# The 1e-9 of two softmaxes as a summed place, and pooled keys and values written once instead of twice

## The chip, the cores and the metric

The kernel runs on one core of a Trainium2 chip. The metric is the device time of one execution in microseconds (us); shorter is better. Five engines work side by side, each through its own queue of instructions in order: TensorE (PE in the profile, its weight loads PEld), VectorE (DVE), ScalarE (ACT), GpSimd (POOL) and SyncE (SP), which here issues the DMAs. They meet at semaphores.

## What is computed

Attention over pooled keys and values, then a soft mixture of experts, then an MLP with a squared ReLU. The change touches the first part and the first normalisation of the second:

```python
k_p = k.reshape(B, H, Sp, 8, D).mean(axis=3)          # B=8, H=8, S=576, Sp=72, D=64
v_p = v.reshape(B, H, Sp, 8, D).mean(axis=3)
scores = (1 / sqrt(D)) * q @ k_p^T                    # 72 scores for each query and head
attn = exp(scores - scores.max(-1))
attn = attn / (attn.sum(-1) + 1e-9)
x = attn @ v_p                                        # 4608 tokens x 512
...
logits = x @ phi                                      # 4608 x 32 slots
d = exp(logits - logits.max(0)); d /= d.sum(0) + 1e-9 # over all tokens
slot_input = d.T @ x                                  # 32 slots, into 8 experts w1, w2
...
x = softmax(logits, over slots) @ slot_out
out = (s * relu(x @ w_in)**2 + b) @ w_out             # 4608 x 512
```

## The kernel before

**Stages.** The program has three parts in time. The attention part, to about 217 us, works on tiles of 128 query rows: four pairs of batch entries (`pr` 0 to 3), nine tiles (`u` 0 to 8) in each, 36 in all. The expert part, to about 265 us, streams `w1` and `w2` through the 32 slot rows. The MLP part runs to the end; it is nearly all matmuls of line 1073. Nothing of the change lies behind the first line of the expert part.

**One tile of attention** goes through stages that the loop calls by letters. `st_A` transposes the queries (L353, ACT copy L355). `st_B` makes the scores (L383 into PSUM tile `sc`), DVE takes the row maximum (L390) and subtracts it into `S` (L393). `st_C` lets ACT take the exponential in place (L397); DVE sums each of the 8 rows of 72 (L401 into `sm`), adds 1e-9 (L402), takes the reciprocal (L404); POOL multiplies `S` by it into the probabilities `P` (L421). `st_D` transposes `P` on PE (L434, L435), `st_E` makes the logits (L457, L464), `st_F` brings them into `L_t` (L480, L482).

**Order.** The order is written by hand: for each step `t` a string of letters in `LOOP` or `FIRST` says in which order the stages of different tiles are put down, and each engine runs its own instructions in that order. A tile's B comes two steps behind its A, C one behind that, D two further on, E and F behind that. `r` advances a `dispatch` generator (the sums over tokens of one batch entry, L538 to L623), `p` a `prep` generator.

**Pooling the keys and values** (`pool_chunk`) is what `prep` runs for the next pair while a pair is worked on, by the table `PLAN1` or `PLAN2`: each pair has three chunks of k and three of v, each handed to DVE or POOL. A chunk is three adds of halves: 512 places to 256 (L246), 256 to 128 (L250), 128 to 64 (L251). The last writes each sum twice, side by side, `[128, 3, 2, 64]`, through a repeated read. `kv_transpose` then transposes 128 columns at a time (L264), so that the same 64 rows stand in the upper and in the lower half of a PSUM bank, and ACT copies the upper half into rows 0 to 63 of `kb_t` (L273) or `vt` (L285) and the lower half into rows 64 to 127. The end of a chunk's third add frees the buffer of the load, and SP can issue the next load into it. In all there are 24 chunks: 11 on DVE, 13 on POOL.

**The tail** of attention (`TAIL`) brings the last two batch entries' sums together: `merge_3` multiplies the three partial sums `z_3` by their weights (L521), adds them (L523), adds 1e-9 (L524), takes the reciprocal (L525) and scales (L526). The last `dispatch` needs that for L607, its matmuls L611 and the slot inputs `siz` (L623), with which the expert part starts at L939. At the end of the tail a buffer named `brief` becomes free for one more load of expert weights.

`S` is a tile of a pool with two buffers, allocated anew for each tile; a subtraction into it waits until POOL has read the tile before last.

Of the kernel before, what the change touches and what calls it, by code (L numbers as in the profile page):

```python
# [10 lines left out]
F32 = mybir.dt.float32  # L11
# [3 lines left out]
ALU = mybir.AluOpType  # L15
# [41 lines left out]
def kernel(  # L57
# [37 lines left out]
    m_all = cpool.tile([128, B, 32], F32, name="m_all")  # L95
    z_all = cpool.tile([128, B, 32], F32, name="z_all")
    si_sum = cpool.tile([128, 4, 32], F32, name="si_sum")
# [134 lines left out]
    for i in range(NPR):  # L232
        nc.gpsimd.memset(L_t[i], -3.0e38)

    pump()
    nc.scalar.activation(out=selrep[:, 0, 0:1], in_=ident[:, 0:1], func=ACTF.Exp)
# [6 lines left out]
    def pool_chunk(nm, pr, c, eng):  # L243

        x = where[nm, pr, c][2]
        eng.tensor_tensor(out=x[:, :, 0:256], in0=x[:, :, 0:256], in1=x[:, :, 256:512], op=ALU.add)  # L246
        yield
        if (nm, pr) not in kvp:
            kvp[nm, pr] = pp1.tile([128, 9, 2, D], F32, tag=f"{nm}p", name=f"{nm}p", bufs=1)
        eng.tensor_tensor(out=x[:, :, 0:128], in0=x[:, :, 0:128], in1=x[:, :, 128:256], op=ALU.add)  # L250
        eng.tensor_tensor(  # L251
            out=kvp[nm, pr][:, 3 * c:3 * c + 3],
            in0=x[:, :, 0:64].unsqueeze(2).to_broadcast([128, 3, 2, D]),
            in1=x[:, :, 64:128].unsqueeze(2).to_broadcast([128, 3, 2, D]),
            op=ALU.add,
        )
        done((nm, pr, c))

    def kv_transpose(nm, pr, c):
# [3 lines left out]
        for i in range(3):  # L263
            nc.tensor.transpose(  # L264
                out=ps[:, 128 * i:128 * i + 128],
                in_=src[:, 3 * c + i].rearrange("p t d -> p (t d)"),
                identity=ident,
            )
        if nm == "k":
            for h2 in range(2):  # L270
# [3 lines left out]
                    out=o.rearrange("p n (g u) -> p g n u", g=3),  # L274
                    in_=ps[r, 0:384].rearrange("p (g n u) -> p g n u", g=3, u=8),
                    func=ACTF.Copy, scale=1.0 / 64,
# [4 lines left out]
        for h2 in range(2):  # L281
            r = slice(64 * h2, 64 * h2 + 64)
            o = vt_t[pr][r].rearrange("p b c x -> p (b c) x")[:, :, 24 * c:24 * c + 24]
            i_ = ps[r, 0:384].rearrange("p (g n t u) -> p g n t u", g=3, n=8, t=2)[:, :, :, h2, :]
            nc.scalar.activation(out=o.rearrange("p n (g u) -> p g n u", g=3), in_=i_, func=ACTF.Copy, scale=1.0 / 8)  # L285
# [79 lines left out]
    def st_B(t):  # L365
# [24 lines left out]
        nc.vector.tensor_reduce(out=mx, in_=scv, axis=AX.X, op=ALU.max)  # L390
        S = sc2.tile([128, 2, 4, KP], F32, tag="S", name="S", bufs=2)
        S_t[t] = S
        nc.vector.tensor_tensor(out=S, in0=scv, in1=mx.unsqueeze(3).to_broadcast([128, 2, 4, KP]), op=ALU.subtract)  # L393

    def st_C(t):
        S = S_t[t]
        nc.scalar.activation(out=S, in_=S, func=ACTF.Exp)  # L397
        pr, u = divmod(t, 9)
        S = S_t.pop(t).rearrange("p x i k -> p (x i) k")
        sm = ap2.tile([128, 8], F32, tag="sm", name="sm")  # L400
        nc.vector.tensor_reduce(out=sm, in_=S, axis=AX.X, op=ALU.add)  # L401
        nc.vector.tensor_scalar(out=sm, in0=sm, scalar1=1e-9, scalar2=None, op0=ALU.add)  # L402
        rs = ap2.tile([128, 8], F32, tag="rs", name="rs")
# [115 lines left out]
    def merge_3():  # L519

        nc.vector.tensor_tensor(out=z_3, in0=z_3, in1=m_3, op=ALU.mult)  # L521
        zt = ap2.tile([128, 32], F32, tag="zd", name="zt")
        nc.vector.tensor_reduce(out=zt, in_=z_3.rearrange("p b s -> p s b"), axis=AX.X, op=ALU.add)  # L523
        nc.vector.tensor_scalar(out=zt, in0=zt, scalar1=1e-9, scalar2=None, op0=ALU.add)  # L524
        nc.vector.reciprocal(out=zt, in_=zt)  # L525
# [672 lines left out]
```

## Time and profile before

| | |
|---|---|
| time before, median of 3 runs | 719.14 us (719.0 to 721.34) |
| the profiled execution | 724.16 us; its span 722.0 us, 2.16 us lie around it |
| PE busy, of the span | 665.4 us (92%) |
| DVE busy | 499.0 us (69%) |
| ACT busy | 411.4 us (57%) |
| POOL busy | 297.3 us (41%) |
| mean granted clock of TensorE | 0.956 of full speed |

The span is the time from the first to the last instruction. The shares of busy time are means over parts with different limits: DVE is busy for 69% of the whole and for 70% to 86% of the attention part. A row of the time line gives start, length, engine, line, operation and tile, and in square brackets how long the engine sat idle before it and what ended that. A row of the chain of waits gives start, length and the instruction to which the end of the program can be followed back. The clock column gives 1.00 for 2.4 GHz and 0.50 for 1.2 GHz.

### The profile page before, as it was taken

How to read it: one execution, taken by the hardware profiler on the slowest of the kernel's cores; microseconds unless marked ns; L12 is line 12 of the kernel's file. 1: busy time of each engine (PE TensorE's matmuls, PEld its weight loads, DVE VectorE, ACT ScalarE, POOL GpSimd, SP SyncE). 2: the span in 40 equal slices, each digit the busy share in tenths (PEclk: the TensorE clock that was granted, in tenths of full speed). 3: DMA queues.
4: the chain of work that ended last, by engine and by line, in shares of the span. 5: the costliest groups of instructions: out<-in, count | busy, mean ns of one | idle time of the engine just before them, and what ended most of it. 6: DMA issues, size and time to landing. Idle time of an engine off the chain costs nothing.

```text
span 722.0 us, 11198 instructions
## 1 busy us (share of the span) xinstructions
PE 665.4 (92%) x4294; PEld 522.2 (72%) x4294; DVE 499.0 (69%) x805; ACT 411.4 (57%) x714; POOL 297.3 (41%) x221
## 2 busy tenths in 40 slices
PE   4677889899899978999999999999999999999997
PEld 3566767677763337778888888878788888888885
DVE  6768788667766297788776797888665765456443
ACT  3454666566433345877566666666665666555552
POOL 3646656532210054356132543345331433899100
PEclk9786999899878997999999999999999999999999
DMA  8997446545296980111011110121100000122322
GB/s 302 376 327 223 177 155 198 196 155 203 94 381 241 391 293 33 59 32 58 28 59 59 59 58 1 53 66 59 59 1 0 1 1 1 63 98 90 99 89 88
DMA packets 41317, 88.87 MB, mean 123 GB/s; under 512 B 6960, under 2 KB 15152, under 8 KB 41264
## 3 DMA queue, kind: packets, MB, share of 16 engines
q1 hardware_dynamic: 41264, 88.16, 35.3%
q8 instruction: 34, 0.56, 0.3%
q14 instruction: 19, 0.16, 0.1%
HBM read 78.71 MB, written 9.44 MB: 122 GB/s over the span
## 4 chain that ended last, share of the span: by engine, by line
PE 73%; DVE 16%; ACT 4%; DMA 2%; POOL 2%; issue 2%; SPq 1%; DVEq 0%; POOLq 0%; ACTq 0%
PE o L1073 52%; PE h L1016 4%; PE sc L383 3%; DVE S L393 2%; DVE mx L390 2%; DVE sm L401 2%; PE l L939 2%; DMA ring<-in_v_dram 1%; PE w L434 1%; ACT S L397 1%; PE w L601 1%; PE so_ps L947 1%; DMA brief<-in_moe_w_dram 1%; PE w L578 1%; PE ct L898 1%
## 5 line engine op out<-in xcount | busy, mean ns | idle before, releaser
L1073 PE MATMUL o<-whi,gh 128*128 128x512 f32 x576 | 229.4, 399 | 2.5 <-DVE gh L1043 2.5
L1073 PE MATMUL o<-whi,gl 128*128 128x512 f32 x576 | 225.5, 392 | 0.8 <-DVE gl L1044 0.7
L1073 PE MATMUL o<-wlo,gh 128*128 128x512 f32 x576 | 225.6, 392 | 0.0
L1025 ACT ACTIVATE r<-h 128x768 f32<-128x768 f32 x95 | 77.2, 813 | 152.7 <-PE h L1016 149.0
L1044 DVE TENSOR_TENSOR gl<-r,gh 128x768 fp32r<-128x768 f32 (+1 forms) x97 | 114.5, 1181 | 63.2 <-ACT gh L1033 62.8
L1086 DVE SCALAR_TENSOR_TENSOR part<-o,sb_t,part 128x512 f32<-128x512 f32 x144 | 99.6, 743 | 50.4 <-PE o L1073 47.8
L1073 PEld LDWEIGHTS o<-whi,gh 128*128 128x128 f32 x576 | 108.8, 189 | 24.1 <-issue 5.8
L1073 PEld LDWEIGHTS o<-wlo,gh 128*128 128x128 f32 x576 | 108.7, 189 | 24.1
L1073 PEld LDWEIGHTS o<-whi,gl 128*128 128x128 f32 x576 | 108.8, 189 | 21.6 <-DVE gl L1044 2.8
L831 POOL TENSOR_TENSOR fr<-fr,xp 128x512 f32<-128x512 f32 x28 | 41.1, 1467 | 183.3 <-ACT fr L830 161.2
L1026 ACT ACTIVATE r<-r 128x768 f32<-128x768 f32 x95 | 80.5, 847 | 3.0
L1033 ACT CAST gh<-r 128x768 fp32r<-128x768 f32 x95 | 79.5, 836 | 2.4
L421 POOL TENSOR_TENSOR P<-S,rs 128x576 f32<-128x576 f32 x32 | 37.3, 1166 | 82.9 <-DVE rs L404 42.0
L1167 POOL TENSOR_TENSOR part<-part,wsum 128x512 f32<-128x512 f32 x36 | 53.3, 1521 | 10.5 <-ACT wsum L1161 10.5
L1016 PE MATMUL h<-cT,S 128*128 128x384 f32 x192 | 49.7, 342 | 0.5 <-DVE S L859 0.5
L383 PE MATMUL sc<-kb,qT 128*128 128x144 f32 x256 | 44.3, 325 | 0.0
L832 POOL TENSOR_TENSOR th<-th,fr 128x512 f32<-128x512 f32 x28 | 43.0, 1537 | 2.2
L1016 PEld LDWEIGHTS h<-cT,S 128*128 128x128 f32 x192 | 36.7, 192 | 8.2 <-DVE S L859 0.7
L390 DVE TENSOR_REDUCE mx<-sc 128x8 f32<-128x576 f32 x36 | 26.4, 734 | 20.6 <-PE sc L383 17.3
L383 PEld LDWEIGHTS sc<-kb,qT 128*128 128x128 f32 x256 | 40.0, 223 | 0.4 <-ACT qT L355 0.2
L401 DVE TENSOR_REDUCE sm<-S 128x8 f32<-128x576 f32 x36 | 27.0, 750 | 18.3 <-ACT S L397 18.2
L397 ACT ACTIVATE S<-S 128x576 f32<-128x576 f32 x36 | 24.5, 682 | 25.2 <-DVE S L393 25.2
(211 smaller groups left out, 910.2 us busy)
## 6 DMA issues: line engine op xcount, KB each, us to landing
ring<-in_moe_w_dram SPq DMA_DIRECT2D x14, 1024.0 KB, 7.6
x<-in_moe_w_dram SPq DMA_DIRECT2D x13, 1024.0 KB, 9.8
raw<-in_moe_w_in_dram SPq DMA_DIRECT2D x8, 1024.0 KB, 5.6
raw<-in_moe_w_out_dram SPq DMA_DIRECT2D x8, 1024.0 KB, 4.9
out_dram<-part SPq DMA_DIRECT2D x32, 256.0 KB, 2.5
ring<-in_q_dram SPq DMA_DIRECT2D x7, 1024.0 KB, 9.6
ring<-in_v_dram SPq DMA_DIRECT2D x9, 768.0 KB, 9.8
ring<-in_k_dram SPq DMA_DIRECT2D x7, 768.0 KB, 7.0
```

Of the source, the lines that this page charges most:

```text
L383: nc.tensor.matmul(out=sc[:, i // 2, 2 * KP * (i % 2):2 * KP * (i % 2) + 2 * KP], lhsT=qT[:, i, :], rhs=kb[:, H * bb + 4 * (j % 2) + i, :] ...
L401: nc.vector.tensor_reduce(out=sm, in_=S, axis=AX.X, op=ALU.add)
L831: nc.gpsimd.tensor_tensor(out=fr, in0=fr, in1=xp, op=ALU.mult)
L832: nc.gpsimd.tensor_tensor(out=th if dst is None else dst, in0=th, in1=fr, op=ALU.add)
L1016: nc.tensor.matmul(out=h[x][:, 0:384] if i == 0 else h[:, x, 0:384], lhsT=Sw_t[f], rhs=cT(c, 384), start=True, stop=True)
L1025: nc.scalar.activation(out=r, in_=h[:, :, 0:384], func=ACTF.Relu)
L1026: nc.scalar.activation(out=r, in_=r, func=ACTF.Square)
L1033: nc.scalar.copy(out=gh_t[i], in_=r)
L1044: nc.vector.tensor_tensor(out=gl[:, x], in0=r[:, x], in1=gh[:, x].bitcast(F32), op=ALU.subtract)
L1073: nc.tensor.matmul(out=o_t[tt], lhsT=l[:, x, 128 * c:128 * c + 128], rhs=r, start=(fi == 0 and n == 0), stop=(fi == GROUPS[g] - 1 and n == 2),
L1086: nc.vector.scalar_tensor_tensor(out=p, in0=o_t[tt], scalar=sb_t[:, 0:1], in1=p, op0=ALU.mult, op1=ALU.add)
L1167: nc.gpsimd.tensor_tensor(out=p, in0=p, in1=wsum, op=ALU.add)
```

## The change

There are two parts. In the first, each row of `S` gets a 73rd place that holds 1e-9. Two fixed buffers of 8 rows of 73 are allocated once and taken in turn; a memset writes the 73rd places at the start, and the subtraction, the exponential and the product touch the first 72 only. The sum takes all 73, so the add of 1e-9 (L402) is gone. In the same way the token sums `z_all` get one more entry that holds 1e-9, `merge_3` adds four entries instead of three, and L524 is gone. In the second, the third add of a chunk writes each sum once, `[128, 3, 64]`; the transposes take 64 columns and fill rows 0 to 63 of the bank, and ACT copies these rows twice: to rows 0 to 63 and to rows 64 to 127. The numbers of copies, transposes and adds stay.

```diff
-    z_all = cpool.tile([128, B, 32], F32, name="z_all")
+    z_all = cpool.tile([128, B + 1, 32], F32, name="z_all")
...
+    S_buf = [sc2.tile([128, 2, 4, KP + 1], F32, name=f"S{i}", bufs=1) for i in range(2)]
+    for S in S_buf:
+        nc.vector.memset(S[:, :, :, KP:KP + 1], 1e-9)
+    nc.vector.memset(z_all[:, B], 1e-9)
...
-            kvp[nm, pr] = pp1.tile([128, 9, 2, D], F32, tag=f"{nm}p", name=f"{nm}p", bufs=1)
+            kvp[nm, pr] = pp1.tile([128, 9, D], F32, tag=f"{nm}p", name=f"{nm}p", bufs=1)
...
         eng.tensor_tensor(
-            out=kvp[nm, pr][:, 3 * c:3 * c + 3],
-            in0=x[:, :, 0:64].unsqueeze(2).to_broadcast([128, 3, 2, D]),
-            in1=x[:, :, 64:128].unsqueeze(2).to_broadcast([128, 3, 2, D]),
-            op=ALU.add,
+            out=kvp[nm, pr][:, 3 * c:3 * c + 3], in0=x[:, :, 0:64], in1=x[:, :, 64:128], op=ALU.add,
         )
...
             nc.tensor.transpose(
-                out=ps[:, 128 * i:128 * i + 128],
-                in_=src[:, 3 * c + i].rearrange("p t d -> p (t d)"),
-                identity=ident,
+                out=ps[0:64, 128 * i:128 * i + 128], in_=src[:, 3 * c + i], identity=ident,
             )
...
-                    in_=ps[r, 0:384].rearrange("p (g n u) -> p g n u", g=3, u=8),
+                    in_=ps[0:64, 0:384].rearrange("p (g n u) -> p g n u", g=3, u=8),
...
-            i_ = ps[r, 0:384].rearrange("p (g n t u) -> p g n t u", g=3, n=8, t=2)[:, :, :, h2, :]
+            i_ = ps[0:64, 0:384].rearrange("p (g n t u) -> p g n t u", g=3, n=8, t=2)[:, :, :, h2, :]
...
-        S = sc2.tile([128, 2, 4, KP], F32, tag="S", name="S", bufs=2)
-        S_t[t] = S
-        nc.vector.tensor_tensor(out=S, in0=scv, in1=mx.unsqueeze(3).to_broadcast([128, 2, 4, KP]), op=ALU.subtract)
+        S_t[t] = S = S_buf[t % 2]
+        nc.vector.tensor_tensor(out=S[:, :, :, 0:KP], in0=scv, in1=mx.unsqueeze(3).to_broadcast([128, 2, 4, KP]), op=ALU.subtract)
...
+        Sk = S[:, :, 0:KP]
+        nc.scalar.activation(out=Sk, in_=Sk, func=ACTF.Exp)
         nc.vector.tensor_reduce(out=sm, in_=S, axis=AX.X, op=ALU.add)
-        nc.vector.tensor_scalar(out=sm, in0=sm, scalar1=1e-9, scalar2=None, op0=ALU.add)
+        S = Sk
...
-        nc.vector.tensor_reduce(out=zt, in_=z_3.rearrange("p b s -> p s b"), axis=AX.X, op=ALU.add)
-        nc.vector.tensor_scalar(out=zt, in0=zt, scalar1=1e-9, scalar2=None, op0=ALU.add)
+        nc.vector.tensor_reduce(out=zt, in_=z_all[:, B - 3:].rearrange("p b s -> p s b"), axis=AX.X, op=ALU.add)
```

DVE's queue in the first pair, around the softmax whose sum runs at 65.8 us (`ring_80` is the load of a v chunk of the next pair, `vp` the pooled v, `sc` the scores in PSUM, `w` a PSUM bank); before, and then now:

```order
L251 TENSOR_TENSOR vp<-ring_80 128x384
L482 TENSOR_REDUCE L_72<-w 128x64
L401 TENSOR_REDUCE sm<-S 128x8
L402 TENSOR_SCALAR sm<-sm 128x8
L404 RECIPROCAL rs<-sm 128x8
L390 TENSOR_REDUCE mx<-sc 128x8
L393 TENSOR_TENSOR S<-sc,mx 128x576
```

```order
L256 TENSOR_TENSOR vp<-ring_80 128x192
L482 TENSOR_REDUCE L_72<-w 128x64
L401 TENSOR_REDUCE sm<-S_131 128x8
L404 RECIPROCAL rs<-sm 128x8
L390 TENSOR_REDUCE mx<-sc 128x8
L392 TENSOR_TENSOR S_132<-sc,mx 128x8x72
```

The add of 1e-9 between sum and reciprocal is gone, the third add of the chunk has half the places, and the rest stands in the same order; `S` has become two named buffers.

DVE's queue at the end of the tail, from the copy of the last token sum on; before, and then now:

```order
L566 COPY z_all<-w 128x32
L521 TENSOR_TENSOR z_all<-z_all,m_all 128x96
L523 TENSOR_REDUCE zt<-z_all 128x32
L524 TENSOR_SCALAR zt<-zt 128x32
L525 RECIPROCAL zt<-zt 128x32
L526 TENSOR_TENSOR m_all<-m_all,zt 128x96
L621 COPY si_all<-w 64x128 x2
L607 TENSOR_TENSOR a<-w,m_all 72x256
```

```order
L565 COPY z_all<-w 128x32
L521 TENSOR_TENSOR z_all<-z_all,m_all 128x96
L523 TENSOR_REDUCE zt<-z_all 128x32
L524 RECIPROCAL zt<-zt 128x32
L525 TENSOR_TENSOR m_all<-m_all,zt 128x96
L620 COPY si_all<-w 64x128 x2
L606 TENSOR_TENSOR a<-w,m_all 72x256
```

One instruction of eight is gone; nothing else moved.

PE's queue in the first pair, around the transposes of a k chunk of the second pair that start at 54.2 us (`P_1` and `P_2` are probabilities, `LT` the logits before their transpose); before, and then now:

```order
L383 MATMUL sc<-kb_123,qT 128x144 x4
L434 MATMUL w<-ident,P_1_103 128x128 x4
L435 MATMUL w<-ident,P_1_103 64x128
L264 MATMUL w<-ident,kp 128x128 x3
L353 MATMUL w<-ident,qm 128x128 x4
```

```order
L383 MATMUL sc<-kb_123,qT 128x144 x4
L434 MATMUL w<-ident,P_1_103 128x128 x4
L435 MATMUL w<-ident,P_1_103 64x128
L266 MATMUL w<-ident,kp 64x128 x3
L353 MATMUL w<-ident,qm 128x128 x4
```

The three transposes give 64 rows instead of 128; their place is the same.

## Rows read from the trace of the kernel before

**Rows 1.** Busy time by stretch: PE, PEld, DVE, ACT, POOL, clock, DMA share, GB/s.

```profile
30.00:60.00 30.00, 24.04 (x213) 19.69 (x212) 20.49 (x38) 16.15 (x38) 13.96 (x12) 0.73 0.88 292
90.00:120.00 30.00, 25.18 (x311) 20.50 (x309) 25.89 (x50) 18.75 (x46) 16.81 (x14) 1.00 0.46 141
150.00:180.00 30.00, 28.66 (x395) 23.42 (x393) 21.62 (x49) 18.48 (x49) 8.05 (x7) 1.00 0.46 170
224.00:250.00 26.00, 26.00 (x202) 8.30 (x194) 8.31 (x27) 10.20 (x38) 0.13 (x1) 1.00 0.94 341
```

**Rows 2.** The chain of waits at the adds of 1e-9: start, length, instruction.

```profile
44.99 0.18 DVE sm L402
...
45.20 0.20 DVE rs L404
...
189.15 0.18 DVE sm L402
```

**Rows 3.** Time line of DVE: a chunk's adds while POOL is idle or past its reads.

```profile
32.88 0.95 DVE L246 TENSOR_TENSOR raw<-raw 128x768 f32<-128x768 f32 x1
34.46 0.56 DVE L251 TENSOR_TENSOR kp<-raw 128x384 f32<-128x384 f32 x1
```

**Rows 4.** Time line of POOL: the first and third add of a chunk.

```profile
47.73 1.00 POOL L251 TENSOR_TENSOR kp<-raw 128x384 f32<-128x384 f32 x1
...
78.70 1.80 POOL L246 TENSOR_TENSOR ring<-ring 128x768 f32<-128x768 f32 x1
```

**Rows 5.** Time lines of DVE and then POOL, both adding a chunk.

```profile
63.05 1.24 DVE L250 TENSOR_TENSOR ring<-ring 128x384 f32<-128x384 f32 x1
64.32 1.23 DVE L251 TENSOR_TENSOR vp<-ring 128x384 f32<-128x384 f32 x1
...
62.23 1.64 POOL L250 TENSOR_TENSOR ring<-ring 128x384 f32<-128x384 f32 x1
63.95 1.19 POOL L251 TENSOR_TENSOR vp<-ring 128x384 f32<-128x384 f32 x1
```

**Rows 6.** The chain of waits at the third adds.

```profile
21.16 1.19 POOL vp L251
...
117.79 1.24 DVE kp L251
...
148.29 1.14 POOL vp L251
```

**Rows 7.** Time line of PE: its waits for DVE and POOL, in brackets.

```profile
27.73 1.12 PE L434 MATMUL w<-ident,Pm 128*128 128x128 f32 x4 [4.30 <-POOL Pm L421]
...
54.21 0.87 PE L264 MATMUL w<-ident,kp 128*128 128x128 f32 x3 [3.12 <-DVE kp L251]
68.87 0.39 PE L545 MATMUL w<-ident,md 128*32 128x128 f32 x1 [4.57 <-DVE md L538]
82.17 0.52 PE L264 MATMUL w<-ident,kp 128*128 128x128 f32 x3 [1.94 <-ACT LT L469]
...
149.47 0.55 PE L264 MATMUL w<-ident,vp 128*128 128x128 f32 x3 [1.27 <-POOL vp L251]
```

**Rows 8.** Groups by line and form, weight loads: count, busy us, mean ns.

```profile
L434 PEld LDWEIGHTS w<-ident,P 128*128 128x128 f32 x128 | 16.7, 158 | 3.8 <-POOL P L421 2.5 <-ACT vps L297 0.4 <-issue 0.3
L435 PEld LDWEIGHTS w<-ident,P 128*64 128x64 f32 x32 | 4.0, 125 | 0.3 <-ACT qT L355 0.3
```

**Rows 9.** Groups by line and form: copies of ACT, and a strided sum of DVE.

```profile
L273 ACT ACTIVATE kb<-w 64x384 f32<-64x384 f32 x24 | 11.7, 488 | 11.7 <-PE w L264 11.5
L587 ACT COPY at<-w 128x288 f32<-128x288 f32 x16 | 6.3, 400 | 2.9 <-PE w L583 2.4
L538 DVE TENSOR_REDUCE md<-L 128x32 f32<-128x160 f32 x8 | 3.2, 406 | 0.1
```

**Rows 10.** The chain of waits at the end of attention.

```profile
212.83 0.19 DVE zt L524
...
216.74 6.72 DMA brief<-in_moe_w_dram
```

More of the change, by code (lines that the diff above doesn't have):

```diff
@@ L390, in st_B @@
         nc.vector.tensor_reduce(out=mx, in_=scv, axis=AX.X, op=ALU.max)
-        S = sc2.tile([128, 2, 4, KP], F32, tag="S", name="S", bufs=2)
-        S_t[t] = S
-        nc.vector.tensor_tensor(out=S, in0=scv, in1=mx.unsqueeze(3).to_broadcast([128, 2, 4, KP]), op=ALU.subtract)
+        S_t[t] = S = S_buf[t % 2]
+        nc.vector.tensor_tensor(out=S[:, :, :, 0:KP], in0=scv, in1=mx.unsqueeze(3).to_broadcast([128, 2, 4, KP]), op=ALU.subtract)
     def st_C(t):
-        S = S_t[t]
-        nc.scalar.activation(out=S, in_=S, func=ACTF.Exp)
+        S = S_t.pop(t).rearrange("p x i k -> p (x i) k")
         pr, u = divmod(t, 9)
-        S = S_t.pop(t).rearrange("p x i k -> p (x i) k")
         sm = ap2.tile([128, 8], F32, tag="sm", name="sm")
+        Sk = S[:, :, 0:KP]
+        nc.scalar.activation(out=Sk, in_=Sk, func=ACTF.Exp)
         nc.vector.tensor_reduce(out=sm, in_=S, axis=AX.X, op=ALU.add)
-        nc.vector.tensor_scalar(out=sm, in0=sm, scalar1=1e-9, scalar2=None, op0=ALU.add)
+        S = Sk
         rs = ap2.tile([128, 8], F32, tag="rs", name="rs")
```

## The prediction

> **What bounds the kernel now.** I read the busy times by stretch first. Between 90 and 120 us PE is busy for 25.2 of 30 us and DVE for 25.9; between 150 and 180 us PE stands at 28.7 and DVE at 21.6 [rows 1]. So no one engine sets the pace of the attention part: PE and DVE hand it to each other, and from about 150 us on PE holds it almost alone. From 224 to 250 us PE is busy without a gap [rows 1], and everything there starts from the slot inputs at the end of attention; the change leaves that part alone, so a gain or a loss in attention moves it as a block. The question is therefore how much earlier attention ends. For that I followed the chain of waits through its 217 us. It passes 17 of the 36 adds of 1e-9 (the first and the last in [rows 2]), nine of the 24 third adds (six on DVE, three on POOL, [rows 3, 5, 6]) and the add of the tail [rows 10]. Then I looked at PE's own waits [rows 7], since what DVE or POOL finish sooner is worth something only where PE would otherwise stand idle.
>
> **The change part by part.**
>
> *The 36 adds of 1e-9.* From the start of such an add to the start of the reciprocal behind it pass 45.20 - 44.99 = 0.21 us [rows 2]. All 36 are 7.6 us of DVE time; the 17 on the chain are 17 x 0.21 = 3.6 us. The sum takes 8 places more: a place costs (0.95 - 0.56) / (768 - 384) = 1.0 ns on DVE [rows 3], so 0.008 us, and 17 of them 0.14 us. The waits of the subtraction stay what they were, since two buffers taken in turn are what the pool gave, and the three memsets at the start stand in DVE's queue ahead of an instruction that waits for POOL anyway, while the first load is still on its way. I cost them at nothing; if that cover were gone they would be three tiny instructions once, under 0.21 us each by [rows 2].
>
> *The third adds.* On DVE 384 places take 0.56 us alone [rows 3], so 192 take 0.56 - 192 x 1.0 ns = 0.36, a gain of 0.20. On POOL a place costs (1.80 - 1.00) / 384 = 2.1 ns [rows 4], a gain of 0.40. When both add a chunk, both stretch: POOL's second add takes 1.64 instead of 1.00, DVE's second and third 1.24 and 1.23 instead of 0.56 [rows 3 to 5]. The ends tell why: DVE's second add ends 64.29, POOL's 63.87; DVE's third ends 65.55, POOL's 65.14. Both times DVE is 0.41 to 0.42 us behind the other's end: it waits for POOL's instruction and then does its own. With both third adds halved, such a pair gains on both sides, 0.40 + 0.20 = 0.6 us. Of the six DVE adds on the chain four are of that kind (1.23 to 1.25; [rows 5] and the 117.79 of [rows 6]) and two free: 4 x 0.6 + 2 x 0.2 = 2.8 us. The lower bound, if only DVE's own places counted, is 6 x 0.2 = 1.2. The three POOL adds on the chain (1.19 the first, 1.14 the last, [rows 6]) give 3 x 0.4 = 1.2.
>
> *Transposes and copies.* A weight load of 64 columns takes 125 ns, one of 128 columns 158 [rows 8]: 72 x 33 ns = 2.4 us of PEld, which runs beside the matmuls, and the moving side keeps its 128 columns. I take zero; the most it can give is the first load behind a wait, some 24 x 0.033 = 0.8 us. ACT makes the same copies of the same size. That a copy leaves the rows it reads is new, and the trace has no row for it. A gain is excluded, since places and instruction stay the same; above, a copy could be held as DVE is in [rows 5], for its own length again, 0.49 us [rows 9], on 24 copies. I take zero, the row of a plain copy being the nearest.
>
> *The tail.* L524 leaves 0.19 + 0.02 us [rows 10], and 32 more strided places cost about 32 x 0.406 / 160 = 0.08 [rows 9]. The load of `brief`, on the chain for 6.72 us behind it, starts from the same end of attention [rows 10]. Net 0.1.
>
> Sum along the chain: 3.6 - 0.14 + 2.8 + 1.2 + 0.1 = 7.6 us. That is the ceiling, as another path can be late next at each handover.
>
> *What is kept.* I go by PE's waits [rows 7]. Ahead of 27.7 us, PE waited 4.30 for POOL, with two third adds on the way: 0.8. Ahead of 54.2 us it waited 3.12, with two adds of 1e-9 and one free third add: 0.6. Ahead of 68.9 us 4.57, with a locked third add and one 1e-9: 0.8. Ahead of 82.2 us 1.94, the same: 0.8. Ahead of 149.5 us 1.27, with a free third add, two 1e-9 and POOL's 0.4: 1.0. In each the wait is longer than what is saved, so I keep it all: 4.0 us. The other 3.6 us lie in stretches (93 to 132 us, 159 to 199 us) where PE's single waits are near 1 us or less and PE's own queue is late next; I keep a quarter, 0.9. Forecast: **4.9 us** less. On the profiled execution this is a span of 717.1 instead of 722.0, and 719.3 with the 2.16 us around it instead of 724.16. That execution was slower than the three timed ones, and 4.9 us is 0.7% of either; from the median 719.14 it gives **714.2 us**.
>
> **The rivals.**
>
> *The whole chain comes through* (7.6 us, 711.5). For it: DVE is busy for 25.9 of 30 us in the middle [rows 1], and what is taken from it also shortens waits on the port that are off the chain. Against it: PE's 28.7 of 30 from 150 us on [rows 1].
>
> *PE and the loads hold the pace.* Between 30 and 60 us the DMA engines are busy 0.88 of the time and the clock is granted at 0.73 on average [rows 1], so the first two items (0.8 + 0.6) could be eaten by the next load or by slower matmuls; PE's run from 150 us eats the 1.0 before it and the 0.9. Then only the two of 0.8 at 68.9 and 82.2 us are left: 1.6 us, 717.5.
>
> *The rows of 73 places are slower to walk* (the side of slower). 73 places are 292 bytes, so rows of `S` no longer follow each other without a gap for the subtraction, the exponential and the product. The trace has no row with this step. The nearest are these: ACT writing runs of 8 places takes 488 ns for 384 places and 400 ns for 288 straight ones, so the 96 further places took 0.92 ns each, less than the mean 1.39 of the straight ones, and the 48 gaps cost next to nothing [rows 9]; DVE reading 160 places at a step of 128 bytes takes 0.406 us [rows 9] where straight ones would take 0.56 - 224 x 1.0 ns = 0.34, which is 0.07 more, or 0.26 for 576 places. At 0.26 us on the subtraction and the exponential of the 17 tiles on the chain it is 34 x 0.26 = 8.8 us, less 4.9: 3.9 us slower, 723.0. It decides from 4.9 / 34 = 0.14 us per instruction. On POOL's product the same price would lengthen PE's wait at 27.7 us [rows 7], once. I think this unlikely, since the nearer row, ACT's, shows nothing.
>
> The Trainium skill (SBUF — State Buffer, Door 1: The DMA port swizzle) speaks on this side: it says SBUF has 16-byte lines and each access that crosses to a new line pays. By it a row of 288 bytes that starts off a line touches 19 lines instead of 18, for three rows in four; as an estimate from that page 4% more, 0.04 us on an instruction of 1 us, which is under the 0.14 at which the gain is lost and would leave the forecast at 715.6 (34 x 0.04 = 1.4). No row of the trace before shows it.
>
> **How the numbers follow.** The forecast, 3 to 6.5 us less around 714.2: 0.52. The whole chain, 711.5: 0.20. PE and loads hold the pace, 717.5: 0.21. Slow rows, 723.0: 0.05; something the trace does not show, ACT's copies across the halves for one, 0.02 on the same side. A measurement of this kernel can tell about 0.3%, 2.2 us, from no change. Faster by more than that: the first two cases and a quarter of the third, 0.77; the same: the rest of the third and a little of the slow ones, 0.17; slower 0.06. The range leaves out the slow cases and a part of each outer one: from 711.0, which takes in the ceiling with half a microsecond of clock, to 719.0, where the PE case with its own uncertainty ends.
>
> **What would show it.** In the profile after: no add of 1e-9; third adds of 0.36 us on DVE and 0.60 on POOL, and about 0.6 where both add at once; subtraction, exponential and product at their old lengths (a rise of 0.14 us is the slow rival); ACT's copies of k still 0.49 us; the weight loads of the 72 transposes near 125 ns and PE no shorter; PE's waits of [rows 7] shorter by what I keep there; the load of `brief` issued near 211.8 us instead of 216.7, and what follows it as long as before. I am wrong if `brief` moves by under 2 us although the adds are gone (then PE's or ACT's waits have taken their place), or if the part behind it changes its length, which would be the clock or the loads and not the sums above.

## The result, and the profile after

The changed kernel takes 712.59 us (median, 711.7 to 714.96), the kernel before beside it 720.24 us: a ratio of 0.9875, with a 95% interval of 0.9848 to 0.9902, or 7.6 us by the medians and 9.0 by the ratio. Taken again later (e11 below) it was 711.94 against 721.77, 0.9853 (0.9819 to 0.9888). The forecast was 714.2, 4.9 us less. The sign and the time are within what was said; the gain is half as large again by the medians and nearly twice as large by the ratio, above the 3 to 6.5 us of the forecast's own case, and lies where the rival "the whole chain comes through" stood (7.6 us).

The page of the changed kernel begins with its span and the busy times (before: 722.0 us; PE 665.4, DVE 499.0, ACT 411.4, POOL 297.3):

```profile
span 710.7 us, 11170 instructions
PE 659.3 (93%) x4294; PEld 515.4 (73%) x4294; DVE 489.3 (69%) x771; ACT 410.1 (58%) x714; POOL 291.4 (41%) x221
```

DVE lost 9.7 us, POOL 5.9. PE lost 6.1 although it has exactly as many instructions and a matmul of the narrowed transposes still takes 273 ns. What differs is the clock: by the mean granted clocks of the two profiles, 0.956 and 0.969, TensorE stood at 1.2 GHz for 64 us of the span before and for 44 after. The clock comes back below.

**Durations.** Time lines of DVE and then POOL after, which answer to [rows 3 to 5]:

```profile
50.78 0.36 DVE L256 TENSOR_TENSOR kp<-raw 128x192 f32<-128x192 f32 x1
...
60.80 0.63 DVE L256 TENSOR_TENSOR vp<-ring 128x192 f32<-128x192 f32 x1
...
45.37 0.60 POOL L256 TENSOR_TENSOR kp<-raw 128x192 f32<-128x192 f32 x1
...
60.43 0.78 POOL L256 TENSOR_TENSOR vp<-ring 128x192 f32<-128x192 f32 x1
```

The free third adds take 0.36 and 0.60 us, to the hundredth what was worked out, and where both add at once DVE takes 0.63 (about 0.6 was said). POOL's ends at 61.21, DVE's at 61.43, 0.22 us behind it. The other touched instructions, by line: count, then shortest, median and longest duration in ns, first and last start, and the shape.

```profile
L392 DVE TENSOR_TENSOR S<-sc,mx x36: 757/758/760, 15.9 to 185.5; 128x576 f32<-128x576 f32 x36
L400 ACT ACTIVATE S<-S x36: 666/684/697, 18.6 to 186.3; 128x576 f32<-128x576 f32 x36
L401 DVE TENSOR_REDUCE sm<-S x36: 746/761/764, 22.6 to 187.7; 128x8 f32<-128x584 f32 x36
L421 POOL TENSOR_TENSOR P<-S,rs x32: 1147/1149/1687, 27.2 to 188.8; 128x576 f32<-128x576 f32 x32
L273 ACT ACTIVATE kb<-w x24: 482/483/498, 8.7 to 134.0; 64x384 f32<-64x384 f32 x24
L266 PEld LDWEIGHTS w<-ident,kp x36: 108/112/177, 7.8 to 132.7; 128*64 128x64 f32 x36
```

Medians before, in the same order: 758, 683, 753, 1149, 486 and 142 ns. So the sum pays 8 ns for its 8 further places, and rows of 73 places and copies from one half of the rows into the other cost nothing.

**Where the time went.** Busy time of PE, PEld, DVE, ACT and POOL, the clock, the DMA share and GB/s in the stretches of [rows 1], and the part behind attention, which was 504.40 us (217.60 to 722.00) before:

```profile
30.00:60.00 30.00, 24.58 (x275) 19.30 (x273) 21.71 (x36) 18.78 (x44) 16.56 (x14) 0.86 0.98 332
90.00:120.00 30.00, 27.15 (x336) 21.78 (x336) 24.43 (x44) 21.12 (x54) 19.57 (x18) 1.00 0.68 227
...
207.30:710.70 503.40, 491.35 (x2416) 379.61 (x2416) 338.65 (x485) 297.09 (x436) 196.90 (x133) 0.99 0.22 76
```

Of the 11.3 us between the two profiled spans 10.3 lie in attention: SP issues the load of `brief` at 206.43 us instead of 216.74, where 211.8 was expected. PE's waits of [rows 7] are now these:

```profile
27.25 0.66 PE L434 MATMUL w<-ident,Pm 128*128 128x128 f32 x4 [3.88 <-POOL Pm L421]
...
51.28 0.49 PE L266 MATMUL w<-ident,kp 128*64 128x128 f32 x3 [2.64 <-DVE kp L256]
64.55 0.40 PE L544 MATMUL w<-ident,md 128*32 128x128 f32 x1 [4.55 <-DVE md L537]
77.03 0.49 PE L266 MATMUL w<-ident,kp 128*64 128x128 f32 x3 [1.52 <-ACT LT L469]
...
139.19 0.52 PE L266 MATMUL w<-ident,vp 128*64 128x128 f32 x3 [2.08 <-POOL vp L256]
```

They start 0.48, 2.93, 4.32, 5.14 and 10.28 us earlier, but the waits themselves changed by -0.42, -0.48, -0.02, -0.42 and +0.81: PE comes to them earlier too. And between the fourth and the fifth, where 1.0 us and a part of the 0.9 were to be kept, 5.1 us were gained.

**A ruler for the middle.** Each of the first six dispatches begins its last third with eight small matmuls that read `sel` (L601 before, L600 after). They cut attention from 82 or 87 us to 181 or 192 us into five strides, each from the start of one such group to the start of the next; I call the earliest stride 0 and the others first to fourth. Time line of PE, before and then after:

```profile
87.47 1.20 PE L601 MATMUL w<-sel,at 128*72 128x32 f32 x16
108.19 1.23 PE L601 MATMUL w<-sel,at 128*72 128x32 f32 x16 [0.37 <-ACT LT L469]
131.98 1.80 PE L601 MATMUL w<-sel,at 128*72 128x32 f32 x16
154.52 1.22 PE L601 MATMUL w<-sel,at 128*72 128x32 f32 x16
175.66 1.23 PE L601 MATMUL w<-sel,at 128*72 128x32 f32 x16
192.41 1.23 PE L601 MATMUL w<-sel,at 128*72 128x32 f32 x16 [0.79 <-ACT LT L469]
```

```profile
82.32 1.20 PE L600 MATMUL w<-sel,at 128*72 128x32 f32 x16
101.84 1.23 PE L600 MATMUL w<-sel,at 128*72 128x32 f32 x16 [0.32 <-ACT LT L469]
124.47 1.23 PE L600 MATMUL w<-sel,at 128*72 128x32 f32 x16
144.21 1.22 PE L600 MATMUL w<-sel,at 128*72 128x32 f32 x16
164.77 1.23 PE L600 MATMUL w<-sel,at 128*72 128x32 f32 x16
180.95 1.60 PE L600 MATMUL w<-sel,at 128*72 128x32 f32 x16 [0.80 <-ACT LT L469]
```

The strides are 20.72, 23.79, 22.54, 21.14 and 16.75 us before, and 19.52, 22.63, 19.74, 20.56 and 16.18 after: 1.20, 1.16, 2.80, 0.58 and 0.57 less. The next one, to the group of the seventh dispatch (208.99 before, 199.18 after), went the other way, from 16.58 to 18.23, and holds 14 us at 1.2 GHz after where it held 10 before. In the experiments the strides repeat to 0.03 us wherever the clock stands still, so they show single hundredths where whole runs differ by microseconds.

**The clock.** In the second stride of before the groups at 131.98 and behind it are slow: the scores of four heads (L383) take 2.27 us there and 1.23 at the same place after. The granted clock of that stride was 0.85 before (half clock, 1.2 GHz, at 132 to 136 and 143 to 146 us) and is 1.00 after. Over the whole of attention TensorE stood at 1.2 GHz for 47 us in the profile of before and 32 in that of after. Single executions of one kernel differ by ten such microseconds, and their times with them: over 170 executions of the fourteen runs told of here, with a level for each run, 1 us more at 1.2 GHz (worked out from the mean granted clock of the execution) goes with 0.22 us more of span (95%: 0.02 each way). "At equal clock" below is a difference from before with this taken off, 95% about 0.9 us each way with six executions and 0.65 with twelve. At equal clock the change gives 7.5 us, and taken again 8.4; the means were 51.5 us at 1.2 GHz before and 45.7 and 44.7 after, so some 1.3 to 1.5 us of the raw gain go with the clock. That the one causes the other is not shown by this.

### The profile page after: what moved, and what is told of

It reads as the page before. It is cut to its first block, busy times and chain, and to the rows that moved or that the text cites. A ratio compares the mean times of both kernels' runs of the same rounds, so it can differ in the third digit from the quotient of the medians.

```text
span 710.7 us, 11170 instructions
## 1 busy us (share of the span) xinstructions
PE 659.3 (93%) x4294; PEld 515.4 (73%) x4294; DVE 489.3 (69%) x771; ACT 410.1 (58%) x714; POOL 291.4 (41%) x221
## 4 chain that ended last, share of the span: by engine, by line
PE 76%; DVE 14%; ACT 4%; POOL 2%; issue 1%; DMA 1%; SPq 1%; DVEq 0%; ACTq 0%; POOLq 0%
PE o L1072 53%; PE h L1015 4%; PE sc L383 3%; PE l L938 2%; DVE S L392 2%; DVE mx L390 2%; PE so_ps L946 2%; DVE sm L401 2%; DMA ring<-in_v_dram 1%; PE w L434 1%; ACT S L400 1%; PE w L600 1%; PE w L577 1%; PE w L353 1%; PE ct L897 1%
## 5 line engine op out<-in xcount | busy, mean ns | idle before, releaser
L1015 PE MATMUL h<-cT,S 128*128 128x384 f32 x192 | 48.8, 336 | 0.5 <-DVE S L858 0.5
L383 PE MATMUL sc<-kb,qT 128*128 128x144 f32 x256 | 42.5, 315 | 0.0
L1015 PEld LDWEIGHTS h<-cT,S 128*128 128x128 f32 x192 | 35.9, 188 | 8.1 <-DVE S L858 0.7
L401 DVE TENSOR_REDUCE sm<-S 128x8 f32<-128x584 f32 x36 | 27.3, 758 | 18.2 <-ACT S L400 18.1
L383 PEld LDWEIGHTS sc<-kb,qT 128*128 128x128 f32 x256 | 38.3, 215 | 0.3 <-ACT qT L355 0.2
```

Of the source, the lines that this page charges most:

```text
L383: nc.tensor.matmul(out=sc[:, i // 2, 2 * KP * (i % 2):2 * KP * (i % 2) + 2 * KP], lhsT=qT[:, i, :], rhs=kb[:, H * bb + 4 * (j % 2) + i, :] ...
L1015: nc.tensor.matmul(out=h[x][:, 0:384] if i == 0 else h[:, x, 0:384], lhsT=Sw_t[f], rhs=cT(c, 384), start=True, stop=True)
```

## The experiments

My theory was the forecast's: the adds and the shorter third adds come off the handovers between DVE, POOL and PE, and in part. The rivals were that only one half of the change works, that rows of 73 places or copies across the halves take something back, that the gain is the clock's, and that the split between long waits and full stretches is not as I made it. The kernel before was timed beside them at 721.57 us (e1 to e4), 721.82 (e5 to e8) and 721.77 (e9 to e12).

### The two halves alone: e1, e2

e1 is the kernel before with the 73rd place and the fourth token sum alone, e2 with the keys and values written once alone:

```diff
+        nc.scalar.activation(out=Sk, in_=Sk, func=ACTF.Exp)
         nc.vector.tensor_reduce(out=sm, in_=S, axis=AX.X, op=ALU.add)
-        nc.vector.tensor_scalar(out=sm, in0=sm, scalar1=1e-9, scalar2=None, op0=ALU.add)
```

```diff
-            out=kvp[nm, pr][:, 3 * c:3 * c + 3],
-            in0=x[:, :, 0:64].unsqueeze(2).to_broadcast([128, 3, 2, D]),
-            in1=x[:, :, 64:128].unsqueeze(2).to_broadcast([128, 3, 2, D]),
+            out=kvp[nm, pr][:, 3 * c:3 * c + 3], in0=x[:, :, 0:64], in1=x[:, :, 64:128], op=ALU.add,
...
-                in_=src[:, 3 * c + i].rearrange("p t d -> p (t d)"),
+                out=ps[0:64, 128 * i:128 * i + 128], in_=src[:, 3 * c + i], identity=ident,
```

> Only the 1e-9 half of the change: rows of 73 places and the fourth token sum, with the pooled keys and values written twice as before. Chain theory (the time that is taken off the chain of waits comes back, as far as PE waits for it): 17 adds of 0.21 us on the chain less 0.14, and 0.1 at the tail, so 3.5 us less at most and about 2.3 less kept. Clock theory (a part of the 10 us by which attention ended earlier in the profile is TensorE running at 2.4 instead of 1.2 GHz): the total can be off from 2.3 to 3.5 us by several us either way, and the difference is found again as a change of the time that attention spends at 1.2 GHz (47 us before, 32 us after, in the two profiles). Slow-row theory: no gain or a loss.

> Only the other half: third adds of half the size, transposes of 64 columns, ACT copying rows 0 to 63 to both halves; the adds of 1e-9 stay. Chain theory: 2.8 us of DVE's and 1.2 us of POOL's third adds on the chain, 4.0 us less at most, about 2.6 kept; with the other half this makes up what the whole change gives. Clock theory: off from that by several us, with the time at 1.2 GHz accounting for it.

e1: 717.74 us, 0.9948 (0.9932 to 0.9964), 3.9 us less at equal clock. e2: 719.53 us, 0.9964 (0.9940 to 0.9988), 2.5 less. Both halves work. The adds give the whole of their 3.6 us on the chain; the third adds alone give 2.5 of 4.0. The two add up to 6.4, the change to 7.5 and 8.4: together they may give a little more than apart, but that lies at the edge of the intervals, and in the strides below the two savings simply add.

### The new layout without its gain: e3, e7

e3 has the rows of 73 places, sums 72 of them and keeps the add. e7 has the narrow transposes and the copies across the halves, while the third add still writes each sum twice:

```diff
+        nc.scalar.activation(out=Sk, in_=Sk, func=ACTF.Exp)
+        nc.vector.tensor_reduce(out=sm, in_=Sk, axis=AX.X, op=ALU.add)
         nc.vector.tensor_scalar(out=sm, in0=sm, scalar1=1e-9, scalar2=None, op0=ALU.add)
```

```diff
-                in_=src[:, 3 * c + i].rearrange("p t d -> p (t d)"),
+                out=ps[0:64, 128 * i:128 * i + 128], in_=src[:, 3 * c + i, 0], identity=ident,
...
-                    in_=ps[r, 0:384].rearrange("p (g n u) -> p g n u", g=3, u=8),
+                    in_=ps[0:64, 0:384].rearrange("p (g n u) -> p g n u", g=3, u=8),
```

> The rows of 73 places and the fourth token sum, but the sum takes 72 places and the add of 1e-9 stays: what the step of 292 bytes and the fixed buffers cost alone. Chain theory: within 0.5 us of the kernel before, and subtraction, exponential and product at 0.76, 0.68 and 1.15 us. Slow-row theory: slower by up to 8.8 us, with these lengths up by 0.14 us or more. Clock theory: may differ from the kernel before by 1 to 3 us although nothing in the lengths differs.

> The kernel before, but the transposes of pooled keys and values take 64 columns (the third add still writes each sum twice, the second copy is not read) and ACT copies rows 0 to 63 to both halves. Prediction's step: nothing, at most 0.8 us less from weight loads behind a wait; ACT's copies keep 0.49 and 0.33 us. Then all of what the keys-and-values half gave, 2.3 us at equal clock, is the shorter third adds. If copies across the halves cost, this run is slower and the third adds gave more than 2.3.

e3: 722.95 us, 1.0005 (0.9984 to 1.0025), 0.1 more at equal clock. e7: 722.8 us, 1.0010 (0.9989 to 1.0032), 0.2 more. Neither layout costs or gives anything that shows (0.7 us either way), and their strides at full clock are those of before (table below). The subtraction, exponential and sum of e3, by line:

```profile
L397 DVE TENSOR_TENSOR S<-sc,mx x36: 757/758/760, 16.1 to 194.8; 128x576 f32<-128x576 f32 x36
L405 ACT ACTIVATE S<-S x36: 666/684/697, 18.0 to 195.6; 128x576 f32<-128x576 f32 x36
L406 DVE TENSOR_REDUCE sm<-S x36: 736/753/754, 22.6 to 196.9; 128x8 f32<-128x576 f32 x36
```

They are the lengths of before (758, 683, 753), and the product in e3 has its 1149 ns. The rival of slow rows is refuted on every one of its instructions. The rule of the Trainium skill (SBUF — State Buffer, Door 1: The DMA port swizzle) on 16-byte lines, from which 0.04 us per instruction were estimated, does not show here: rows of 288 bytes at a step of 292 cost 0 to 1 ns.

### Making the add longer: e4

```diff
         nc.vector.tensor_scalar(out=sm, in0=sm, scalar1=1e-9, scalar2=None, op0=ALU.add)
+        nc.vector.tensor_scalar(out=sm, in0=sm, scalar1=1e-9, scalar2=None, op0=ALU.add)
```

> The kernel before with the add of 1e-9 written twice, 36 more instructions of 0.21 us on VectorE (the row sum gets 2e-9; the last digits of the output change by nothing that can be seen). Chain theory: at least the 17 on the chain, 3.6 us slower, at most all 36, 7.6 us slower, since a longer path pulls further instructions onto the chain. Clock theory: more or less than that by what the time at 1.2 GHz changes. If a quarter of it or less shows (under 1 us), VectorE does not bound the middle of attention.

726.14 us, 1.0077 (1.0053 to 1.0101), 5.1 us more at equal clock. This lies between the 3.6 of the 17 on the chain and the 7.6 of all 36. Removing them gave 3.9, and with 0.9 us either way on both the two numbers alone do not differ. In the strides at full clock (the ruler above) the longer adds cost 0.59, 1.02 and 0.61 us in stride 0, the first and the fourth, where removing them (e1) gave 0.61, 0.59 and 0.58: in one stride of three more of them come onto the path when they grow than were on it before.

### Which tiles pay: e5, e6, e9, e10

The forecast kept all in front of the long waits and a quarter in the stretches of 93 to 132 and 159 to 199 us. The sums of tiles 13 to 20 and 26 to 34 lie in these stretches ("the middle": 11 adds on the chain, 2.3 us); the other 19 tiles hold 6 (1.3 us). e5 is e1 with the add left out only in the middle, e6 with it left out only in the others. e9 and e10 do the same from the other side, in the changed kernel: e9 has the add put back in the 19 others, e10 in the 17 of the middle. The edit of e5 and e9; e6 and e10 have `if not (...)`:

```diff
-        nc.vector.tensor_reduce(out=sm, in_=S, axis=AX.X, op=ALU.add)
+        if 13 <= t <= 20 or 26 <= t <= 34:
+            nc.vector.tensor_reduce(out=sm, in_=S, axis=AX.X, op=ALU.add)
+        else:
+            nc.vector.tensor_reduce(out=sm, in_=Sk, axis=AX.X, op=ALU.add)
+            nc.vector.tensor_scalar(out=sm, in0=sm, scalar1=1e-9, scalar2=None, op0=ALU.add)
```

> As the first run (rows of 73 places, keys and values as before), but the add of 1e-9 is left out only in the 17 tiles whose sums run from 93 to 132 us and from 159 to 199 us, where the prediction kept a quarter because TensorE's single waits there are near 1 us or less; the other 19 tiles keep it. 11 of the 17 adds are on the chain of waits, 2.3 us. Prediction's step: a quarter, 0.6 us less. If the whole chain comes back: 2.3 us less, and if the adds beside the chain count too, up to 3.6. TensorE's time at 1.2 GHz of each run is taken into account.

> The complement of the run before: the add of 1e-9 is left out in the other 19 tiles and kept in those 17. 6 of these 19 are on the chain, 1.3 us. Prediction's step: all of it, 1.3 us less. The two runs together should give what the first run gave, 3.7 us at equal clock; if this one gives less than the other, the prediction had the two sorts of stretches the wrong way round.

> The changed kernel with the add of 1e-9 put back in 19 tiles and left out only in the 17 whose sums run from 93 to 132 and from 159 to 199 us. If gains of parts simply add: the keys-and-values half at equal clock, 2.4 us less than before, and 1.3 for these tiles, so 3.7. If the parts help each other (each alone is in part taken up by the path that the other would shorten): more, 4.5 to 6.

> The changed kernel with the add of 1e-9 put back in those 17 tiles and left out in the other 19. If gains simply add: 2.4 and 0.75, so 3.2 us less than before at equal clock. If the parts help each other: 4 to 6. The changed kernel gives 7.4.

> The changed kernel again, on the chip of the runs beside it: 7 to 9 us less than before, 7.4 of it at equal clock.

| kernel | add left out in | third adds | median us | ratio to before (95%) | at equal clock |
|---|---|---|---|---|---|
| e5 | middle | old | 720.53 | 0.9975 (0.9950 to 0.9999) | -1.3 |
| e6 | others | old | 720.61 | 0.9980 (0.9951 to 1.0009) | -0.8 |
| e9 | middle | halved | 713.63 | 0.9887 (0.9847 to 0.9927) | -7.0 |
| e10 | others | halved | 716.13 | 0.9911 (0.9879 to 0.9943) | -5.2 |
| e11 | all (the change again) | halved | 711.94 | 0.9853 (0.9819 to 0.9888) | -8.4 |

At equal clock the whole runs lean one way: putting the adds back costs 2.3 to 3.2 us in the middle (from the 7.5 and the 8.4), but 0.5 to 1.4 in the others. e5 and e6 alone differ by less than their intervals. The ruler decides for what lies between 82 or 87 and 181 or 192 us. PE's groups in e10:

```profile
103.17 1.23 PE L604 MATMUL w<-sel,at 128*72 128x32 f32 x16 [0.51 <-ACT LT L473]
126.38 1.23 PE L604 MATMUL w<-sel,at 128*72 128x32 f32 x16
147.68 1.22 PE L604 MATMUL w<-sel,at 128*72 128x32 f32 x16
168.79 1.23 PE L604 MATMUL w<-sel,at 128*72 128x32 f32 x16
185.55 1.23 PE L604 MATMUL w<-sel,at 128*72 128x32 f32 x16 [0.78 <-ACT LT L473]
```

The strides of all, from the same groups of each kernel (an asterisk: part of it at 1.2 GHz):

| kernel | stride 0 | first | second | third | fourth |
|---|---|---|---|---|---|
| before | 20.72 | 23.79 | 22.54* | 21.14 | 16.75 |
| e3, rows of 73 and the add | 20.70 | 23.79 | 22.43* | 21.14 | 16.76 |
| e7, narrow transposes alone | 20.69 | 23.78 | 20.76* | 21.13 | 16.76 |
| e6, add left out in the others | 20.70 | 23.79 | 21.81* | 21.13 | 16.75 |
| e2, third adds halved | 20.10 | 23.22 | 21.74* | 21.12 | 16.74 |
| e1, all adds gone | 20.11 | 23.20 | 22.03* | 20.56 | 16.17 |
| e5, add left out in the middle | 20.13 | 23.20 | 22.33* | 20.55 | 16.17 |
| e10, third adds halved, add left out in the others | 20.10 | 23.21 | 21.30* | 21.11 | 16.76 |
| e9, third adds halved, add left out in the middle | 19.52 | 22.63 | 20.13 | 20.56 | 16.16 |
| after | 19.52 | 22.63 | 19.74 | 20.56 | 16.18 |
| e11, after again | 19.51 | 22.63 | 19.73 | 20.55 | 16.16 |

Stride 0 and the first, third and fourth know only two causes. Each loses 0.55 to 0.60 us when the adds of the middle go, whether the third adds are halved or not, and nothing when the others go. That is three tiles' worth of 0.21 - 0.008 = 0.20 us in each, of the four or five tiles whose sums lie in a stride. Stride 0 and the first lose 0.57 to 0.62 more when the third adds are halved: each has one locked pair on the chain (at 97.54 us, and the 117.79 us of [rows 6]), priced at 0.6. No quarter is to be seen: all that the chain passes is kept, 1.20 + 1.16 + 0.58 + 0.57 = 3.5 us.

In the second stride the other adds (tiles 21 to 25 lie there) cost 0.39 us, the difference between e9 and after at full clock. How much of its 2.80 us is the clock can be read from e7, whose adds and third adds are those of before. Busy times and clock of this stride, in before and then in e7:

```profile
131.98:154.52 22.54, 19.36 (x176) 16.03 (x176) 14.22 (x34) 12.50 (x32) 10.41 (x9) 0.85 0.51 192
```

```profile
132.75:153.51 20.76, 17.78 (x177) 14.89 (x177) 14.20 (x34) 12.21 (x32) 10.28 (x9) 0.92 0.56 208
```

Before was at 1.2 GHz there twice, e7 once (143 to 146 us), and e7 is 1.78 us shorter with the same work. Its one stretch, 10 us behind the start, may cost nothing: e12 (below) had 3.4 us at 1.2 GHz at the same place and took 19.74, as after did at full clock. By this some 1.8 of the 2.80 us are the clock and 1.0 the change, of which 0.39 are the adds and the rest would be the third adds at 138.64 and 148.29 us; the forecast had 1.0 there. In other kernels of the table the same 3.4 us stood 16 us behind the start, and there the stride is longer.

Why nothing was lost shows in PE's busy time. The stretches of the first stride, and of the third and fourth together, before and then after:

```profile
108.19:131.98 23.79, 21.57 (x294) 17.29 (x294) 19.72 (x40) 16.00 (x41) 16.21 (x13) 1.00 0.70 236
...
154.52:192.41 37.89, 34.05 (x447) 27.97 (x446) 28.61 (x67) 22.31 (x57) 10.34 (x9) 1.00 0.40 140
```

```profile
101.84:124.47 22.63, 21.37 (x295) 17.14 (x295) 18.31 (x35) 15.98 (x41) 14.97 (x13) 1.00 0.71 249
...
144.21:180.95 36.74, 33.80 (x446) 27.92 (x446) 27.18 (x58) 22.46 (x57) 10.34 (x9) 1.00 0.41 145
```

PE idled 23.79 - 21.57 = 2.22 us and 37.89 - 34.05 = 3.84 us there before, each in pieces of about 1 us or less, and 1.26 and 2.94 after. The idle time fell by 0.96 and 0.90 us of the 1.16 and 1.15 gained. The waits were short, but there were enough of them. Single ones fell by one add each; PE's wait for `md` in the third stride and for `P` in the fourth, before and then after:

```profile
163.29 0.28 PE L545 MATMUL w<-ident,md 128*32 128x128 f32 x1 [1.09 <-DVE md L538]
...
190.93 0.44 PE L434 MATMUL w<-ident,P 128*128 128x128 f32 x2 [0.65 <-POOL P L421]
```

```profile
152.77 0.28 PE L544 MATMUL w<-ident,md 128*32 128x128 f32 x1 [0.89 <-DVE md L537]
...
179.46 0.44 PE L434 MATMUL w<-ident,P 128*128 128x128 f32 x2 [0.45 <-POOL P L421]
```

The wait for `md` in the first stride fell likewise, from 1.04 to 0.84, and one in the fourth from 0.41 to 0.21. Others, such as the 0.79 for `LT` ahead of the last group, stayed.

### The clock as a cause: e8, e12

If the half clock were what makes the difference, unread matmuls in PE's longest waits should bring time. `fill` writes 128x128 products of `ident` that the next instruction overwrites, into the bank that the waiting instruction is to use: in e8 24 ahead of the wait at 64.55 us and 8 ahead of the `sel` group at 180.95, in e12 18 and, for the second place, 3 ahead of the matmul of the token sum that stands just before it (L564).

```diff
+    def fill(ps, n):
+        for _ in range(n):
+            nc.tensor.matmul(out=ps[:, 0:128], lhsT=ident, rhs=ident, start=True, stop=True)
...
         ps = bank()
+        fill(ps, FILL0 if b_ == 0 else 0)
         nc.tensor.transpose(out=ps[0:32, 0:128], in_=md, identity=ident)
```

> The changed kernel with 32 matmuls that nobody reads: 24 of 128x128 just before TensorE's wait for the first dispatch (the wait of 4.55 us at 60 us) and 8 before its wait of 0.80 us at 180 us, behind which it ran at 1.2 GHz for 8 and 14 us in the profile. Clock theory: the time at 1.2 GHz falls by 8 to 20 us, and the run is 0.2 to 0.3 us faster for each of them, 2 to 5 us. Chain theory: no faster, up to 1 us slower where the matmuls overrun the waits.

> The changed kernel with 18 unread matmuls before the first dispatch's wait instead of 24, and 3 placed ahead of the wait at 180 us, before the matmul of the token sum, instead of 8 behind it; 0.23 us each by the run with 32. Clock theory: time at 1.2 GHz 8 to 12 us less than in the changed kernel, at 0.22 us for each some 2 to 2.5 us faster, as these matmuls now fit into the waits. Chain theory: the same time as the changed kernel.

e8: 714.43 us, 0.9907 (0.9876 to 0.9937). Its eight at the second place came only behind the 0.81 us of the wait, which is for the same bank, and took 2.05 us themselves; its first 24 took 5.62 us where the wait had been 4.55. So e8 prices extra matmuls more than the clock. e12 put them where PE idled: 711.94 us, 0.9864 (0.9831 to 0.9898), the same as the changed kernel beside it (e11), with a mean of 38.6 us at 1.2 GHz instead of 44.7. At 0.22 each that should have brought 1.3 us; by the means e12 is 0.8 us slower, with 2.0 us either way, so that 1.3 is only just outside of what these runs allow. What became of it stands in two places of its time line of PE, and in the part behind attention:

```profile
179.97 0.83 PE L536 MATMUL w<-ident 128*128 128x128 f32 x6
181.07 1.23 PE L607 MATMUL w<-sel,at 128*72 128x32 f32 x16
182.13 1.23 PE L384 MATMUL sc<-kb,qT 128*128 128x144 f32 x8
...
186.58 0.27 PE L550 MATMUL w<-ident,md 128*32 128x128 f32 x1 [1.61 <-DVE md L542]
...
211.15 1.06 PE L945 MATMUL l<-brief,siz 128*32 128x512 f32 x8 [0.50 <-DMA brief<-in_moe_w_dram]
```

```profile
204.95:709.80 504.85, 491.19 (x2416) 380.19 (x2416) 339.16 (x485) 297.23 (x436) 197.03 (x133) 0.98 0.22 76
```

The changed kernel at the same place, at half clock from 182 us:

```profile
182.36 2.27 PE L383 MATMUL sc<-kb,qT 128*128 128x144 f32 x8
...
187.92 0.37 PE L544 MATMUL w<-ident,md 128*32 128x128 f32 x1 [0.20 <-DVE md L537]
```

With full clock the scores take 1.23 us instead of 2.27, and PE is at the sum over tokens 1.3 us sooner (186.58 against 187.92) after waiting 1.61 us for DVE there instead of 0.20. The expert part starts 2.35 us earlier (204.95 against 207.30). It is then 1.45 us longer (504.85 against 503.40). Little of that is the load of `brief`: from the start of the expert part to the matmuls that wait for it pass 6.20 us in e12 and 5.92 in the changed kernel, and the DMA engines are as busy in both (0.97 and 0.95 of the time from 187 to 208 us). Up to the matmuls of L988 (L981 in the changed kernel), near the end of the expert part, e12 is even 1.41 us quicker than the changed kernel, 46.97 against 48.38. The loss comes behind them, up to the third group of L1022 (L1015), where the MLP part begins; e12 and then the changed kernel:

```profile
251.92:271.16 19.24, 14.25 (x64) 10.94 (x65) 15.64 (x21) 9.65 (x18) 10.39 (x9) 0.73 0.28 98
```

```profile
255.68:272.16 16.48, 12.56 (x64) 9.81 (x65) 13.40 (x19) 9.58 (x18) 8.68 (x8) 0.90 0.20 72
```

The same work takes 2.76 us longer there at a granted clock of 0.73 instead of 0.90, that is 10 us at 1.2 GHz instead of 3. So in this profile the unread matmuls won time from the clock in attention, and a part of it was lost to the clock again behind it. That is two profiles; over the timed runs no gain is to be seen. The clock does change the length of single stretches, but that the 1.3 to 1.5 us that go with it in the comparison with before are caused by it is not shown, and neither is what a better clock throughout would bring.

No kernel tried is faster than the changed one.

## Why the prediction was right, and where it was not

- **What the parts take off.** Right to the hundredth: the free third adds, the sum, the copies, the subtraction. A locked pair gave 0.57 to 0.62 in the strides for the 0.6 said. That DVE "waits for POOL's instruction and then does its own" can't be quite the mechanism: it ended 0.41 to 0.42 us behind POOL before, where its own add takes 0.56, and 0.22 after, where it takes 0.36. The transposes' weight loads fell by 30 ns to 112, not to 125, since they took 142 and not the 158 of another line; worth nothing that shows, as said (e7).
- **The sum along the chain, 7.6 us.** This is what arrived: 7.5 and 8.4 us at equal clock. The count of adds on the chain is not exact place by place: in the third stride the chain of before passed only one (161.00 us), and 0.58 us, three adds' worth, came off. In the first it passed four and three came off; in stride 0 and the fourth it passed three, and three came off.
- **What is kept: the step that failed.** "PE's single waits are near 1 us or less and PE's own queue is late next; I keep a quarter, 0.9" is refuted for all that the ruler measures. The four strides that cover most of those stretches gave 3.5 of the 3.6 us, at full clock before and after, where 0.9 was forecast. So the time came into the range because the range took in the rival's 7.6 us, with more than a microsecond that goes with the clock, and not because the forecast's own case came true. A short wait keeps what is saved as long as it is longer than that, and 0.2 us per tile is no more than the 0.2 to 1 us of these waits; I compared single waits with the sum of all savings.
- **The four waits up to 82 us**, 3.0 us by the forecast, gave 5.1 in the pair of profiles, although the waits themselves fell by 1.3 only. Why it is more stays open. There were 27 us at 1.2 GHz in it before and 17 after, which at 0.22 would be the difference, but e12 had 14 and reached its second `sel` group no earlier (101.97 against 101.84). This part also scatters more than the strides: the first `sel` group came at 87.47 us in before and at 86.28 and 88.28 in e3 and e7, whose work there costs the same, and at 82.32 and 82.91 in the two profiles of the changed kernel. So the gain up to there is between 3.4 and 6.0 us, depending on which profiles are compared.
- **The wait at 149 us**, 1.0 us by the forecast. The second stride, in which it lies, gave 2.8; by e7 some 1.8 of them are the clock and 1.0 the change. It fits that in before the `sel` group, scores and their neighbours up to 137.02 us took 5.04 us, and after, at full clock, 3.40 (124.47 to 127.87).
- **The part behind attention** is 1.0 us shorter in the pair of profiles, where it was to stay; it holds 12 us at 1.2 GHz after instead of 16. PE and loads as the pace: refuted on this change (DMA share 0.98 instead of 0.88 between 30 and 60 us, and no stride at full clock lost).
- **Slow rows, slow copies**: refuted by e3 and e7.

## What to carry to other kernels

Where two engines pass each tile to and fro, a saving per tile can be kept whole if it is no larger than the short wait of that tile, as it was here for three of the four or five tiles of a stride; look at the idle time of the limiting engine summed over the stretch, not at its longest single waits. Find landmarks that recur (here one group of matmuls per batch entry) and compare strides between them at equal clock: they resolve hundredths of a microsecond where whole runs scatter by several. A constant that must be added behind a sum can stand as one more place in what is summed, and a value needed in two places can be copied by an engine that copies anyway, if the longer row and the odd copy are found to be free, as they were here.

## What the runs showed of the hardware

- After two waits of 0.45 and 0.80 us PE ran at a granted clock of 0.50 from about 182 to 195 us in the changed kernel while it was busy almost without a gap; the scores of four heads took 2.27 us instead of 1.15 seven microseconds before.
- Rows of 72 fp32 places at a step of 292 bytes run at the speed of straight ones: 758 ns on DVE, 684 on ACT, 1149 on POOL.
- ACT reads PSUM rows 0 to 63 and writes SBUF rows 64 to 127 in the time of a straight copy: 483 ns for 384 places.
- What 3.4 us at 1.2 GHz cost depends on where they lie: the second stride took 19.74 us with them 10 us behind its start (e12), 21.36 with them 16 us behind it (e8), and 19.74 without any (the changed kernel).
